# An order of instructions recomputed from other transfer times, with a margin behind landings

## The chip, the cores and the metric

The kernel runs on one core of one Trainium2 chip. The metric is the device time of one execution in microseconds; smaller is better. Three timed runs of the kernel before gave 565.68, 567.0 and 568.76 us; their median, 567.0 us, is the time before.

A core has five engines, each with an instruction queue of its own that is worked off in order: TensorE (PE in the profile, with its weight loads as PEld), VectorE (DVE), ScalarE (ACT), GpSimd (POOL) and SyncE (SP). In this kernel SP does nothing but start transfers. An instruction can wait for a semaphore; while it waits, everything behind it on the same queue waits too.

## The reference

Two equal layers on `x` of 2048 tokens by 640 features, in bfloat16. Each layer normalises, does a segmented attention with a running memory, adds, normalises, does a ReLU feed-forward of width 1728, and adds:

```
x = x + A(layernorm(x))      # 32 heads of 20, 4 segments of 512 tokens
x = x + relu(layernorm(x) @ w1) @ w2
x = x + A(layernorm(x))
x = x + relu(layernorm(x) @ w1) @ w2

# A, for each segment s with q, k, v of 32 heads:
p     = softmax(q k^T * 20**-0.5 + causal mask)
a_dot = p v
a_mem = (phi(q) M) / (phi(q) z + 1e-6)
o     = sigmoid(beta) * a_mem + (1 - sigmoid(beta)) * a_dot
M     = M + phi(k)^T v ;  z = z + sum(phi(k))       # phi(t) = t + 1 or exp(t)
out   = concat(o) @ wo
```

## The kernel before

All weights and the whole of `x` stay on the core. The work is cut by layer (2), by segment (4 of 512 tokens) and, within attention, by pairs of head groups: a group is four heads, so a segment has eight groups and four pairs, and the whole kernel has 32 pairs, counted m = 0 to 31. A pair's scores are made in five rounds of two halves each; a half fills two banks of PSUM, ACT takes the exponential of it (L1155), and POOL cuts the causal triangle (L1167). PE then multiplies by the values (L1197 in the first segment, L1246 after it). Between these, PE does the projections of later segments (L640 is the first matmul of each accumulation group, L643 the others), the reads and updates of the running memory (L996, L1047), the output projection and the feed-forward. A few matmuls of the identity (L623 at the start, L627 later) compute nothing: they keep PE's clock up where it is expected to have nothing else.

Three kinds of transfer sit between the engines, nearly all of them started from SP. Queries and keys are copied from `stg` to DRAM (`spill`, L889) and read back with heads on other partitions into one of three `pad` buffers (`fill`, L934); only the first pair is copied on the chip (`first_heads`, L913). Transposes (`turn`, L671) turn normalised tokens, attention values (`avt`), head outputs (`oT`) and `phi(k)`; SP holds its queue for each of them. The loads of the weights come in pieces (`late_loads`, L528 to L546); `w2` is loaded into a region that the first segments use for other data until their last memory read (L996 with `w_r`), so its pieces wait for that.

The order of the instructions is not written by hand. Every step is a stream that yields operations (`Op`), and `Sched.run` merges the streams when the program is built. It keeps a clock for each engine and a time for each result. In each turn it takes from the heads of all streams the one with the smallest `round(start + late)`: `start` is when the engine is free and the awaited results are there by its own costs, and `late` is a penalty that moves an operation back in the choice but not in its time. Already there before: for a PE operation of a stream that is not first in rank, a result that came from a transfer counts only 1000 ns after its recorded landing (`TRUST_NS`). Where a planned gap of PE is 300 ns or more, `keep_busy` fills it with identity matmuls. A transfer's recorded landing is the end of its issue (or the end of the transfers before it) plus `lat`.

The whole plan is made for 32 values of the assumed cost of a change of PE's tiling (`STARTS`: 97 ns, up and down in steps of 0.75). `late(seed)` then replays each order with random extra landing times (mean `LATE_NS`, 300 ns), and the order with the smallest sum over four seeds is the one that is emitted. On the chip nothing of this is left but the order on each queue and the semaphores: no instruction waits for a planned time.

Of the kernel before, what the change touches and what calls it, by code (L numbers as in the profile page):

```python
# [18 lines left out]
FC = D // 128  # L19
# [140 lines left out]
SWITCH_NS = 97.0  # L160
STARTS = [SWITCH_NS + 0.75 * (k - 32 // 2) for k in range(32)]
LATE_NS = 300.0
JOIN_NS = 4000.0
SEM_NS = 60.0
PE_MARGIN = 80.0
IDLE_NS = 300.0
COLD_NS = 8000.0
TRUST_NS = {"dma": 1000.0, "pool": 400.0, "act": 400.0, "dve": 400.0, "pe": 0.0}
# [4 lines left out]
class Sched:  # L173
# [93 lines left out]
    def run(self):  # L267
        while True:
# [22 lines left out]
            for prio, n, st, alts, op, late in heads:  # L291
# [4 lines left out]
                if prio > 0 and alts and alts[0][3] == "pe":  # L296
                    sl = self._pick(op.acq).tks if op.acq is not None else []
                    sure = max([self.at(t) + TRUST_NS[self.P.lane(t)] for t in op.waits + sl], default=0.0)
                    late = max(late, sure - alts[0][1])
                for end, start, k, e in alts:  # L300
                    if not any(p2 < min(prio, HOLDERS) and st2 is not st
                               and any(e2 == e and s2 + HOLD_TOL[e] < end for _, s2, _, e2 in al2[:1])
                               for p2, _, st2, al2, _, _ in heads):
                        ok.append((end, start, k))
# [30 lines left out]
            if op.dma is not None:  # L335
                tk = self.P.dma(e, fns[0][0], op.dma)
                self.dma_free = max(self.dma_free, start + 300.0) + tail[1]
                self.t[(id(tk[0]), tk[1])] = max(self.dma_free, end) + tail[0]
                if tail[2]:
# [13 lines left out]
    def late(self, seed):  # L353
# [5 lines left out]
        for e, hold, tail, waits, out, is_dma in self.log:  # L359
            m = SEM_NS + (PE_MARGIN if e == "pe" else 0.0)  # L360
            start = max([t[id(k[0]), k[1]] + m for k in waits], default=0.0)
            start = max(free[e], start)
            free[e] = start + hold
            if is_dma:
                dma_free = max(dma_free, start + 300.0) + tail[1]
                land = max(dma_free, free[e]) + tail[0] + rnd.expovariate(1.0 / LATE_NS)
                if tail[2]:
                    free[e] = max(free[e], dma_free)
# [39 lines left out]
def plan(switch, sb, sem_, psum, dram, A_x, A_wq, A_wk, A_wv, A_wo, A_beta, B_x, B_w1, B_w2, out):  # L408
# [86 lines left out]
    def ld(e, name, nbytes, fn, waits=()):  # L495
        tk = yield dma(e, sem_("d_" + name), nbytes, fn, waits, lat=2200.0)
        S.set(name, tks=[tk])
# [26 lines left out]
    def late_loads():  # L524
# [27 lines left out]
        for n, (name, nbytes, fn) in enumerate(pieces):  # L552
# [3 lines left out]
            if n == n2:  # L556
                v0 = yield Need("v00")
                q1 = yield Need("q01")
                w2w = v0 + q1 + early_done
            tk = yield dma("sp", sems[name], nbytes, fn, w[:1] + (w2w if n >= n2 else []) + z1, issue=400.0, lat=4500.0)  # L560
            left[name] -= 1
# [105 lines left out]

    def turn(slot_sem, dst, src, waits):

        n = src.shape[-1] // 128  # L670
        tk = yield dma("sp", slot_sem, 32768 * n, lambda e: e.dma_start_transpose(dst, src), waits,  # L671
                       issue=max(1400.0, 140.0 * n), lat=2000.0, rate=270.0, holds=True)
        return tk

    def lnorm(s, x_tks, pool_, parts=1):
# [3 lines left out]
        for p0 in range(0, 4, n):  # L679
# [11 lines left out]
            for i in range(p0, p0 + n, 2):  # L691
# [5 lines left out]
                t1 = yield dve(D, 4, lambda e, bx=bx, t=t: nm(e, bx, t, 1), [tch], extra=120)  # L697
                tT = yield from turn(xn_sem[id(bx)], xt.ap[:, i * FC:(i + 2) * FC, :], bx.ap, [t0, t1] + xt.tks)
                bx.release(tT)
# [563 lines left out]
    def turn_av(m):  # L1263
        ev = yield Need("av", m)
        sl, ev = ev[0], ev[1:]
        at = yield Acq([AVT])
        tT = yield from turn(avt_sem, at.ap, sl.ap.rearrange("p z t -> p (z t)"), ev + at.tks)
        sl.release(tT)
# [54 lines left out]
    def turn_o(a, s):  # L1323
        ow = yield Need("oseg", a, s)
        turned = []
        for k in range(2):
            ot = yield Acq([OT[k]])
            ot.users = []
            tT = yield from turn(ot_sem[id(ot)], ot.ap, o_sb[:, 2 * k:2 * k + 2, :].rearrange(
                "p i d -> p (i d)"), ow + ot.tks)  # L1330
            turned.append(tT)
# [19 lines left out]
    def ln_b(p):  # L1351
        def f(a, s):
# [18 lines left out]
            for k in range(2):  # L1371
                tk = yield normed(t0 + k, k, bx, tch)
                tn.append(tk)
            tT = yield from turn(xn_sem[id(bx)], xt.ap[:, 2 * p * FC:(2 * p + 2) * FC, :], bx.ap, tn + xt.tks)
            bx.release(tT)
# [190 lines left out]
```

## Time and profile before

| what | value |
|---|---|
| timed runs, median (lowest, highest) | 567.0 us (565.68, 568.76) |
| profiled execution, its own time | 565.3 us |
| its span, first to last instruction | 563.5 us |
| PE busy | 556.4 us (99%), 5219 matmuls |
| DVE busy | 420.1 us (75%) |
| ACT busy | 404.2 us (72%) |
| POOL busy | 195.1 us (35%) |
| granted TensorE clock | 1.000 |
| bytes moved | 60.93 MB, mean 108 GB/s |

The profiled execution is at the fast end of the runs: 1.7 us under their median. A busy PE is not PE at its peak: matmuls overlap, and a gap between two of them that is shorter than the last one takes to drain is counted as busy. So small losses of PE are read from the starts of its instructions in the timeline, and only waits that outlast the drain show as idle.

### The profile page before, as it was taken

To read this page: it belongs to the slowest core of one execution; us is meant where nothing else is said; L and a number is where in the kernel's file an instruction comes from. 1 tells how busy PE (TensorE), PEld (TensorE's weight loads), DVE (VectorE), ACT (ScalarE), POOL (GpSimd) and SP (SyncE) were. 2 spreads that over 40 slices of the span, in tenths; PEclk is the share of its full clock that TensorE was granted. 3 is DMA by queue.
4 is the path that set the end of the run, shared out by engine and by line. 5 is a ranking of instruction groups with operands and counts; after the bars stand their busy time and mean duration, and the time that the engine had idled before them with its cause. 6 is when DMAs were issued, how large, how long until landed. Compare 5 with 4: busy or idle time off the path is not lost.

```text
span 563.5 us, 12875 instructions
## 1 busy us (share of the span) xinstructions
PE 556.4 (99%) x5219; PEld 305.0 (54%) x5219; DVE 420.1 (75%) x1070; ACT 404.2 (72%) x512; POOL 195.1 (35%) x302
## 2 busy tenths in 40 slices
PE   8999999999999999999999999999999999999998
PEld 7664555445554454645446544555445654665655
DVE  6989789888999689878898997688747964560202
ACT  4789998987788878778986688778878678113140
POOL 4544344333344335444433443035322433110000
PEclk9999999999999999999999999999999999999999
DMA  8695988383474136542375131880326410512101
GB/s 268 120 221 138 238 218 182 74 224 56 97 171 94 44 88 159 118 95 72 92 163 115 27 66 26 193 148 20 67 80 173 109 43 20 116 45 48 47 1 47
DMA packets 130109, 60.93 MB, mean 108 GB/s; under 512 B 108930, under 2 KB 119938, under 8 KB 130050
## 3 DMA queue, kind: packets, MB, share of 16 engines
q1 hardware_dynamic: 129830, 59.85, 45.5%
q8 instruction: 41, 0.67, 0.5%
q10 hardware_dynamic: 220, 0.26, 0.2%
q14 instruction: 18, 0.15, 0.1%
HBM read 20.57 MB, written 12.85 MB: 59 GB/s over the span
## 4 chain that ended last, share of the span: by engine, by line
PE 87%; DVE 8%; DMA 2%; ACT 1%; SPq 1%; issue 0%
PE ps L643 56%; PE ps L640 11%; PE ps L1103 8%; PE ps L1246 6%; DVE stats L651 2%; PE ps L996 2%; PE ps L1197 1%; PE ps L1047 1%; DVE x_sb L1317 1%; PE ps L1394 1%; DMA avt<-av 1%; DVE xn_tok L705 1%; SPq L913 1%; DMA oT<-o_sb 1%; ACT PT L1155 1%; DVE stg L816 1%
## 5 line engine op out<-in xcount | busy, mean ns | idle before, releaser
L1155 ACT ACTIVATE PT<-ps 128x1024 bf16<-128x1024 f32 x320 | 310.0, 1022 | 70.3 <-PE ps L1103 64.6
L1167 POOL TENSOR_SCALAR_AFFINE_SELECT PT<-PT 128x512 bf16<-128x512 bf16 x256 | 166.6, 668 | 268.2 <-ACT PT L1155 267.9
L643 PE MATMUL ps<-w_r,hT 128*128 128x320 bf16 (+2 forms) x768 | 123.0, 299 | 0.0
L643 PE MATMUL ps<-xnT,w_r 128*128 128x512 bf16 x416 | 113.3, 379 | 0.0
L1317 DVE TENSOR_TENSOR x_sb<-x_sb,ps 128x320 bf16<-128x320 bf16 (+1 forms) x128 | 60.3, 479 | 66.7 <-PE ps L643 66.0
L643 PEld LDWEIGHTS ps<-w_r,hT 128*128 128x128 bf16 x768 | 72.4, 98 | 31.9 <-issue 4.4
L1425 ACT ACTIVATE hT<-ps 128x512 bf16<-128x512 f32 x55 | 32.7, 598 | 50.0 <-PE ps L643 49.7
L1103 PE MATMUL ps<-pad 20*128 20x128 bf16 (+3 forms) x1024 | 64.8, 301 | 1.6 <-ACT PT L1155 0.9
L643 PEld LDWEIGHTS ps<-xnT,w_r 128*128 128x128 bf16 x416 | 39.7, 98 | 44.0 <-issue 3.2
L651 DVE BATCH_NORM_STATS2 stats<-x_sb 128x6 f32<-128x320 bf16 x126 | 56.4, 472 | 2.1 <-DMA x_sb<-in_A_x_dram 1.8
L1254 DVE CAST av<-ps 128x512 bf16<-128x512 f32 x53 | 36.2, 684 | 14.8 <-PE ps L1246 14.7
L1103 PEld LDWEIGHTS ps<-pad 20*128 20x128 bf16 x1024 | 18.3, 92 | 52.6 <-ACT PT L1155 25.6
L643 PE MATMUL ps<-wo_r,oT 128*128 128x320 bf16 x256 | 46.1, 299 | 0.0
L1246 PE MATMUL ps<-PT,v_aug 128*32 128x256 bf16 (+5 forms) x896 | 40.7, 302 | 0.0
L1423 DVE TENSOR_SCALAR hT<-ps 128x512 bf16<-128x512 f32 x49 | 33.4, 683 | 9.1 <-PE ps L643 9.0
L640 PE MATMUL ps<-xnT,w_r 128*128 128x512 bf16 x104 | 39.6, 380 | 0.0
L643 PE MATMUL ps<-wv_r,xnT 128*128 128x320 bf16 x192 | 36.7, 300 | 0.0
L643 PE MATMUL ps<-xnT,wk_r 128*128 128x512 bf16 (+1 forms) x140 | 36.1, 349 | 0.0
L643 PE MATMUL ps<-xnT,wq_r 128*128 128x512 bf16 (+1 forms) x140 | 34.9, 349 | 0.0
L665 POOL TENSOR_TENSOR rstd<-lnU,mhalf 128x2 f32<-128x2 f32 (+2 forms) x25 | 20.8, 831 | 38.0 <-DVE lnU L661 34.4
L816 DVE CAST stg<-ps 128x512 bf16<-128x512 f32 (+1 forms) x48 | 29.5, 618 | 3.3 <-PE ps L643 3.2
L1290 DVE TENSOR_TENSOR o_sb<-avt,rden 128x320 bf16<-128x320 bf16 x56 | 30.5, 562 | 0.6
(117 smaller groups left out, 695.8 us busy)
## 6 DMA issues: line engine op xcount, KB each, us to landing
pad<-scr SPq DMA_DIRECT2D x124, 80.0 KB
scr<-stg SPq DMA_DIRECT2D x34, 256.0 KB, 2.9
out_dram<-x_sb SPq DMA_DIRECT2D x15, 160.0 KB, 1.8
w_r<-in_B_w_dram SPq DMA_DIRECT2D x10, 216.0 KB, 4.2
w_r<-in_B_w_dram SPq DMA_DIRECT2D x13, 160.0 KB, 2.8
x_sb<-in_A_x_dram SPq DMA_DIRECT2D x9, 160.0 KB, 2.8
scr<-w_r SPq DMA_DIRECT2D x5, 256.0 KB, 3.6
x_sb<-in_A_x_dram SPq DMA_DIRECT2D x3, 320.0 KB, 7.2
```

The costliest lines, as they stand in the source:

```text
L640: bk, tk = yield pe(mm_ns(n), [(lambda e, bk, a=a, b=b: e.matmul(bk.ap[:, 0:n] if len(b.shape) == 2 else bk.ap[:, 0:n].rearrange("p (i n) ...
L643: tk = yield pe(mm_ns(n), [(lambda e, k=k, a=a, b=b, bk=bk: e.matmul(bk.ap[:, 0:n] if len(b.shape) == 2 else bk.ap[:, 0:n].rearrange("p (i ...
L651: tk = yield dve(320, 1, lambda e, c2=c2: e.bn_stats(stats6[:, t, c2, :], x_sb[:, t, c2 * 320:(c2 + 1) * 320]), xt)
L816: te = yield evac(N, 1, lambda e, sg=sg, bk=bk: e.tensor_copy(sg.ap[:, t0:t0 + N], bk.ap[:, 0:N]), lambda e, sg=sg, bk=bk: e.activation(sg ...
L1103: fns.append([(lambda e, z=z, j=j, hh=hh, N=N, o=o, sl=sl: e.matmul(ps[:, hh, o:o + N], sl.ap[32 * hh:32 * hh + DH, z, 0, 128 * j:128 * j ...
L1155: tx = yield act(1024, lambda e, dst=dst, src=src: e.activation(dst, src, ACT.Exp, scale=SCALE), sc + pw)
L1167: tm = yield pool(600.0, lambda e, reg=reg: e.affine_select(out=reg, in_=reg, pattern=[[0, 4], [1, 128]], compare_op=ALU.is_ge, fill=0.0, ...
L1246: fns.append((lambda e, bk, j=j, hh=hh, pt=pt, g=g0 + z: e.matmul(bk.ap[32 * hh:32 * hh + wide(g, hh), 128 * j:L], VAUG[vx(a, s)][:, j].re ...
L1254: te = yield evac(L, 1, lambda e, sl=sl, z=z, bk=bk: e.tensor_copy(sl.ap[:, z], bk.ap), lambda e, sl=sl, z=z, bk=bk: e.activation(sl.ap[:, ...
L1317: ta = yield dve(n, 1, lambda e: e.tensor_tensor(x_sb[:, t, c0:c0 + n], x_sb[:, t, c0:c0 + n], bk.ap[:, 0:n], ALU.add), [tk] + list(waits) ...
L1423: th = yield evac(512, 1, lambda e, dc=dc, bk=bk: e.tensor_scalar(hT[:, dc, :], bk.ap[:, :], 0.0, None, ALU.max), lambda e, dc=dc, bk=bk: ...
L1425: lambda e, dc=dc, bk=bk: e.activation(hT[:, dc, :], bk.ap[:, :], ACT.Relu), [tk] + HT.tks)
```

## The change

Only numbers of the planner change, and what it does with them; no step of the computation is added or removed.

- Transfer times: the loads at the start get a `lat` each (1500 to 3800 ns, where all had 2200), the late pieces 3500 instead of 4500, the transposes of normalised tokens and of head outputs 2400 and those of attention values 1600, where all had 2000.
- A transfer started between 8 and 106 us is recorded as landing 600 ns later (`EARLY_NS`), and the random replay adds a further random delay of that mean to it.
- A margin: where the first choice of engine of an operation is ACT or DVE and it waits for a transfer, it is penalised in the choice if it would start less than 800 ns (`SURE_NS`) behind the recorded landing.
- The replay charges 1000 ns (`COOL_NS`) for each wait of PE of over 800 ns after the first 10 us.
- The plans tried are 48 instead of 32.

```diff
-STARTS = [SWITCH_NS + 0.75 * (k - 32 // 2) for k in range(32)]
+STARTS = [SWITCH_NS + 0.75 * (k - 48 // 2) for k in range(48)]
+SURE_NS = 800.0
+EARLY_NS = 600.0
+LOADS_NS = 106e3
+COOL_NS = 1000.0
...
+                if alts and alts[0][3] in ("act", "dve"):
+                    sure = max([self.at(t) for t in op.waits if self.P.lane(t) == "dma"], default=0.0)
+                    late = max(late, sure + SURE_NS - alts[0][1])
...
-                self.t[(id(tk[0]), tk[1])] = max(self.dma_free, end) + tail[0]
+                self.t[(id(tk[0]), tk[1])] = max(self.dma_free, end) + tail[0] + (EARLY_NS if 8e3 < start < LOADS_NS else 0.0)
...
+            if e == 'pe' and start - free[e] > 800.0 and start > 10e3:
+                start += COOL_NS
...
+                if 8e3 < start < LOADS_NS:
+                    land += rnd.expovariate(1.0 / EARLY_NS)
...
-        tk = yield dma(e, sem_("d_" + name), nbytes, fn, waits, lat=2200.0)
+        tk = yield dma(e, sem_("d_" + name), nbytes, fn, waits, lat={"x0a": 1950.0, "x0b": 1950.0, "x01": 1500.0, "wk0": 2900.0, "wq0": 2900.0, "wk1": 2900.0, "wq1": 2500.0, "wv": 2200.0, "x10": 3800.0, "x11": 3800.0}.get(name, 2200.0))
...
-            tk = yield dma("sp", sems[name], nbytes, fn, w[:1] + (w2w if n >= n2 else []) + z1, issue=400.0, lat=4500.0)
+            tk = yield dma("sp", sems[name], nbytes, fn, w[:1] + (w2w if n >= n2 else []) + z1, issue=400.0, lat=3500.0)
...
-                tT = yield from turn(xn_sem[id(bx)], xt.ap[:, i * FC:(i + 2) * FC, :], bx.ap, [t0, t1] + xt.tks)
+                tT = yield from turn(xn_sem[id(bx)], xt.ap[:, i * FC:(i + 2) * FC, :], bx.ap, [t0, t1] + xt.tks, lat=2400.0)
...
-        tT = yield from turn(avt_sem, at.ap, sl.ap.rearrange("p z t -> p (z t)"), ev + at.tks)
+        tT = yield from turn(avt_sem, at.ap, sl.ap.rearrange("p z t -> p (z t)"), ev + at.tks, lat=1600.0)
```

The transposes in `turn_o` and `ln_b` get `lat=2400.0` in the same way. The lines of the kernel after stand 11 further down than those of before.

More of the change, by code (lines that the diff above doesn't have):

```diff
@@ L666, in chain, with turn @@
         return tk
-    def turn(slot_sem, dst, src, waits):
+    def turn(slot_sem, dst, src, waits, lat=2000.0):
         n = src.shape[-1] // 128
         tk = yield dma("sp", slot_sem, 32768 * n, lambda e: e.dma_start_transpose(dst, src), waits,
-                       issue=max(1400.0, 140.0 * n), lat=2000.0, rate=270.0, holds=True)
+                       issue=max(1400.0, 140.0 * n), lat=lat, rate=270.0, holds=True)
         return tk
@@ L1329, in turn_o @@
             tT = yield from turn(ot_sem[id(ot)], ot.ap, o_sb[:, 2 * k:2 * k + 2, :].rearrange(
-                "p i d -> p (i d)"), ow + ot.tks)
+                "p i d -> p (i d)"), ow + ot.tks, lat=2400.0)
             turned.append(tT)
@@ L1373, in f @@
                 tn.append(tk)
-            tT = yield from turn(xn_sem[id(bx)], xt.ap[:, 2 * p * FC:(2 * p + 2) * FC, :], bx.ap, tn + xt.tks)
+            tT = yield from turn(xn_sem[id(bx)], xt.ap[:, 2 * p * FC:(2 * p + 2) * FC, :], bx.ap, tn + xt.tks, lat=2400.0)
             bx.release(tT)
```

## The prediction

> **What bounds the kernel now.** I read the page first, then the table of stages, then who waited for whom on PE, then the timeline.
>
> ```profile
> PE 556.4 (99%) x5219; PEld 305.0 (54%) x5219; DVE 420.1 (75%) x1070; ACT 404.2 (72%) x512; POOL 195.1 (35%) x302
> PE 87%; DVE 8%; DMA 2%; ACT 1%; SPq 1%; issue 0%
> ```
>
> PE is busy nearly always and carries 87% of the chain that ended last; transfers carry 2%. The work of PE is the same before and after, so the order can only change what PE loses between its matmuls.
>
> ```profile
> 19.30:80.00 60.70, 60.63 (x740) 34.91 (x740) 54.11 (x148) 55.59 (x74) 26.34 (x39) 1.00 0.82 196
> 80.00:105.10 25.10, 24.05 (x258) 13.37 (x258) 22.62 (x65) 22.57 (x29) 10.57 (x18) 1.00 0.80 168
> 183.00:480.00 297.00, 296.73 (x2763) 153.48 (x2763) 233.87 (x576) 236.61 (x288) 113.88 (x173) 1.00 0.40 91
> ```
>
> Columns after the stage's length: busy PE, PEld, DVE, ACT, POOL, granted clock (1.00: full), DMA share, GB/s. From 183 us on PE idles 0.27 us in 297. The one stage with a visible loss behind the start is 80 to 105 us (1.05 us idle), where DVE and ACT are 90% busy.
>
> ```profile
> PE ps L1103 <- ACT PT L1155: 0.9, 3, 0.4
> PE ps L1103 <- DMA pad<-stg: 0.6, 1, 0.6
> PE ps L640 <- DVE av L1254: 0.4, 2, 0.2
> PE ps L996 <- DVE om_sb L1007: 0.2, 1, 0.2
> PE ps L640 <- DMA oT<-o_sb: 0.2, 1, 0.2
> ```
>
> These are all waits of PE from 12 us to the end: 2.3 us, of which transfers 0.8. That is all that truer transfer times can win outright, 0.4% of 565.
>
> **The prices of PE's order**, from the timeline (start, length, what):
>
> ```profile
> 76.77 0.71 PE L1197 MATMUL ps<-w_r,PT 128*128 128x21 bf16 x22
> 77.55 1.02 PE L643 MATMUL ps<-hT,wq_r 128*128 128x512 bf16 x4
> 78.51 0.39 PE L1103 MATMUL ps<-pad 20*128 20x256 bf16 x4
> 78.83 0.39 PE L640 MATMUL ps<-hT,wq_r 128*128 128x512 bf16 x1
> 80.34 1.40 PE L627 MATMUL ps<-ident 128*128 128x128 bf16 x22
> 84.00 0.31 PE L640 MATMUL ps<-wo_r,oT 128*128 128x320 bf16 x1 [0.21 <-DMA oT<-o_sb]
> ```
>
> Four matmuls of 512 columns, 1.02 us with a last one of 0.38: a step of (1.02 - 0.38)/3 = 0.21 us. The last starts at 77.55 + 0.64 = 78.19, the scores at 78.51, 0.32 later: the change of tiling costs about 0.10. The way back: two runs of 256 columns, at half of 0.21 each, 0.21 together, and 0.32 until 78.83: again 0.10. Filling matmuls: 22 in 1.40 us, and 0.219 for one alone, (1.40 - 0.22)/21 = 0.056 each.
>
> **The change, part by part.** It adds no instruction of work, no wait and no transfer; all its terms come from comparing the two orders, which I did by counting, without times from the planner.
>
> *Fills and tilings.* Behind the start (from the first value projection on) the order before has 39 filling matmuls, the one after 56: 22 and 6 near 80 us, 3 near 113, 8 near 450 become 15 and 14 near 105, 6 near 131, 3, and 18 near 460. Seventeen more at 0.056 are **+0.95 us**; PE runs them whether or not what follows is late. Changes of tiling rise from 393 to 399: six at 0.10, **+0.6 us**. Neither has cover: both stand on PE.
>
> *The start.* These are the rows that it rests on.
>
> ```profile
> 8.08 0.70 POOL L765 TENSOR_TENSOR rstd<-lnU,mhalf 128x2 f32<-128x2 f32 x1 [1.11 <-DVE lnU L763]
> 8.24 0.49 DVE L734 COPY xnT<-ps 128x640 bf16<-128x640 bf16 x1 [0.24 <-PE ps L728]
> 8.88 0.27 PE L640 MATMUL ps<-xnT,wk_r 128*128 128x256 bf16 x1
> 8.98 0.60 PE L643 MATMUL ps<-xnT,wk_r 128*128 128x256 bf16 x4
> 10.03 0.44 PE L728 MATMUL ps<-ident,xn_tok 128*128 128x128 bf16 x5
> 12.78 1.42 DVE L956 TENSOR_SCALAR rtmp<-stg 128x512 bf16<-128x512 bf16 x1 [1.78 <-ACT stg L817]
> 13.02 1.04 POOL L586 MEMSET maskg<- 128x756 bf16 x1
> 13.80 0.30 PE L640 MATMUL ps<-wv_r,xnT 128*128 128x320 bf16 x1
> 14.12 0.41 DVE L816 CAST stg<-ps 128x256 bf16<-128x256 f32 x1
> 14.62 4.73 SPq L913 DMA_DIRECT2D pad<-stg  x6
> 18.41 0.27 PE L640 MATMUL ps<-xnT,wk_r 128*128 128x256 bf16 x1
> 19.30 0.40 PE L1103 MATMUL ps<-pad 20*128 20x512 bf16 x4 [0.62 <-DMA pad<-stg]
> ```
>
> Before, PE starts projecting at 8.88, between the transposes of the second two tiles (the last at 10.03). After, all four transposes stand ahead of the first projection, and on DVE the statistics of tile 3 stand ahead of the first normalisation. The second pair is bound by the same `rstd` (8.78) and one copy (0.49), so its last transpose still comes at about 10; eight groups of five steps of (0.60 - 0.27)/3 = 0.11, 4.4 us, then end at 14.6 to 14.7 instead of 13.80: 0.86 late. Fifteen fills that stood ahead of 8.88 are gone, but PE waits there instead.
>
> Most of it comes back at the first scores. Before, PE has 36 matmuls from 13.80 on, the last at 18.41 lasting a step of 0.11, so it loses 0.78 until the scores at 19.30, whose operands come by transfers issued from 14.62 on. After, 42 matmuls stand there, 5.3 us, and PE arrives at about 19.95. Those transfers do not move as PE does: their issue waits for the cast at 14.12, which is behind a 1.42 us `rtmp`, which ends 0.14 behind POOL's memset. The memset starts as before, so I put the issue at 14.75 and the operands at 19.4: nothing is lost. Net: 0.86 - 0.78, **+0.1 us**. What the old wait hid: nothing late is behind it, since the read-back of the first pair's second half is first asked for some 4 us later.
>
> ```profile
> L956 DVE TENSOR_SCALAR rtmp<-stg x50: 223/285/1423, 12.8 to 433.7; 128x512 bf16<-128x512 bf16 x50
> ```
>
> The same instruction takes 285 ns at the median and 1423 once, beside that memset. The Trainium skill (SBUF — State Buffer, section "SBUF: two separate sides") says that such a VectorE instruction and GpSimd share a port pair as an exclusive lock, held for the whole instruction. By that rule the start follows POOL and the issue is at 14.75; if instead the 1.42 us were its own, all would shift by 0.86, the operands would be there at 20.15, and 0.2 us more would be lost. The row fits the rule, and the sum above does not need it: it takes the end of the memset from the rows.
>
> *The load stage, 20 to 106 us.* Every in-order exponential on ACT stands between PE and its next score bank.
>
> ```profile
> 19.72 1.94 ACT L1155 ACTIVATE PT<-ps 128x1024 bf16<-128x1024 f32 x2 [1.12 <-PE ps L1103]
> 21.55 0.45 ACT L868 ACTIVATE w_r<-ps 128x320 bf16<-128x320 f32 x1
> 21.86 0.64 ACT L963 ACTIVATE phs<-stg 128x512 bf16<-128x512 bf16 x1
> 24.79 0.39 ACT L817 ACTIVATE stg<-ps 128x256 bf16<-128x256 f32 x1
> 25.05 0.64 ACT L963 ACTIVATE phs<-stg 128x512 bf16<-128x512 bf16 x1
> 25.57 1.95 ACT L1155 ACTIVATE PT<-ps 128x1024 bf16<-128x1024 f32 x2
> ```
>
> From start to start: two exponentials 1.83, a value cast 0.31, a small cast 0.26, a phi exponential 0.52. Counting both orders for the first pair of head groups (first exponential to the eleventh): before ten exponentials, 4, 1 and 3 of the others, 12.2 us; after 3, 3 and 3, 12.4. PE's own steps from the first score of this pair to that of the next add up to 14.0 before and 13.0 after. For pair 4 they are 12.3 before and 12.4 after, and ACT's share goes from 4 phi exponentials (11.2) to 5 and two casts (12.4). ACT has no slack left there. Bounds: it costs nothing if ACT runs without a gap, and 1.9 us if it idles as in the row of 19.3 to 80 us (5.1 of 60.7, 8.4%: 12.4/0.916 is 13.5 against 13.0 and 12.4, so 0.6 and 1.1, and pair 3, with 12.1 against 13.1, 0.1). I take **+0.4 us**, near the lower end, because that stage shows PE waiting for 0.07 us in all.
>
> *The wait for `oT` at 84.00 goes.* Its matmul stands 8.7 us of PE's steps behind the last values of the segment (L1197), where before it was reached 6.7 us behind them on the clock (they end their issue at about 77.3): **-0.2 us**. The 80 to 105 us stage else keeps its late casts (DVE and ACT decide them), so I leave its loss as it is; next late there is `av` on DVE.
>
> *SP's queue.* The transposes' and pieces' places move. The heaviest move: ten of `w2`'s pieces went out together before, ahead of one attention transpose and one of `phi(k)`; after, all but the last go ahead of them.
>
> ```profile
> 114.12 4.62 SPq L532 DMA_DIRECT2D w_r<-in_B_w_dram  x10
> 132.03 0.30 PE L640 MATMUL ps<-w_r,hT 128*128 128x320 bf16 x1
> w_u<-in_B_w_dram SPq DMA_DIRECT2D x1, 80.0 KB, 3.7
> 124.42 0.59 SPq L546 DMA_DIRECT2D w_u<-in_B_w_dram  x1
> ```
>
> The last piece landed at 124.42 + 3.7 = 128.1 and was used at 132.03: 3.9 us of slack. After, PE has about 2.7 us fewer steps from the last memory read of that region to this matmul: 1.2 us are left. **0.** The transpose behind four more pieces of 0.46 is up to 1.8 us later, and only a division on DVE reads it.
>
> *Sum.* 0.95 + 0.6 + 0.1 + 0.4 - 0.2 = +1.85 us on the profiled 565.3 (span 563.5 and 1.8 around it): 567.1. The median of the runs lies 1.7 above that execution, so against it I say **568.8 us**, 0.3% above 567.0, within the 0.5% (2.8 us) that a measurement here can tell from no change.
>
> **The rivals.**
> - *The margin pays (0.14).* Waits for transfers and what follows them vanish, in slow runs as in fast ones: all 2.3 us of waits above less the 0.8 already counted, and the 1.7 us between profile and median: 568.8 - 0.4 - 1.5 - 1.7 = 565.2. For it: the runs spread by 3 us. Against it: only 0.8 of the waits name a transfer. It ends below 564.2 only with a better start too.
> - *ACT decides the load stage (0.26): slower.* The idle time of the row of 19.3 to 80 us is needed in each pair: 1.9 instead of 0.4, **570.3**, and with the spread of the runs up to 572. It decides from about 1.4 us on. For it: zero slack in pair 4; against it: PE's 0.07 us of idle there before.
> - *`w2` or a transpose late behind SP (0.07).* Once the 1.2 us are used, each us later is a us of PE; with the 1.8 us behind four pieces on top of a wait as long as the slack, some 570.5.
> - *The clock falls (0.03).* The start shows the price:
>
> ```profile
> 1.58 4.28 PE L623 MATMUL ps<-ident 128*128 128x128 bf16 x43 [1.58 <-POOL mhalf L576]
> ```
>
> 43 matmuls at (4.28 - 0.31)/42 = 0.095 instead of 0.056: 1.7 us. With a wait longer than any in the trace (over 0.7) that is 571.5 or more. The Trainium skill (TensorE: Matmul & The Clock Gate, section "Part 1: The HAM clock gate") puts the re-throttling behind an idle window of about 3.4 us; by that page the time would be some 574. No wait of the trace comes near it, and the clock column of the stages agrees.
> - *The orders do not differ where it counts*: excluded, they differ nearly throughout.
>
> **How the numbers follow.** The forecast itself has 0.50. It ends within 0.5% mostly (0.39), else slower (0.10). The margin paying gives 0.10 same and 0.04 faster; ACT 0.05 same and 0.21 slower; the others 0.10 slower. Faster 0.05, same 0.54, slower 0.41. Range: from 565.2, the first rival, to 572.5, ACT's upper end and the clock's; the likeliest alone 566.5 to 570.5.
>
> **What would show it.** First value projection near 14.6 us and no wait at the first scores; 56 fills behind it; no wait for `oT`; PE waiting for L1155 near 75 to 90 us at most some tenths; the `w2` matmul without a wait. I am wrong if PE's waits behind 12 us sum to under 1 or over 4 us, or the start is not later.

## The result, and the profile after

The kernel after takes 569.01 us (median of 10 runs, 567.63 to 569.91), the kernel before 566.22 in the runs beside it. The ratio is 1.0044, with a 95% interval of 1.003 to 1.0057: by that, 2.5 us (0.44%) slower. The profiled execution of the kernel after spans 567.3 us, 3.8 more than the profiled one of before (563.5).

Page of the kernel after: busy time of the engines, the queue of instruction packets (packets, MB, share), the chain that ended last.

```profile
PE 557.2 (98%) x5223; PEld 305.4 (54%) x5224; DVE 415.1 (73%) x1067; ACT 405.6 (72%) x515; POOL 194.7 (34%) x302
q8 instruction: 41, 0.67, 0.5%
PE 80%; DVE 12%; DMA 3%; ACT 3%; issue 1%; SPq 0%; POOL 0%
```

PE still carries the chain, but its share falls from 87 to 80% and DVE's rises from 8 to 12%. The next two fences give the table of stages of after and, for those stages that were not shown before, of the kernel before (columns as in the prediction).

```profile
80.00:106.00 26.00, 25.96 (x268) 13.82 (x266) 24.90 (x71) 23.30 (x31) 11.12 (x18) 1.00 0.70 178
106.00:183.00 77.00, 75.20 (x720) 38.07 (x717) 63.78 (x164) 62.31 (x74) 32.31 (x48) 1.00 0.52 119
183.00:250.00 67.00, 65.70 (x647) 34.38 (x648) 55.49 (x139) 52.14 (x62) 26.44 (x40) 1.00 0.43 94
250.00:480.00 230.00, 228.76 (x2119) 118.51 (x2118) 177.99 (x446) 181.92 (x223) 85.43 (x133) 1.00 0.42 91
```

```profile
106.00:183.00 77.00, 76.56 (x750) 39.22 (x748) 69.99 (x181) 62.52 (x74) 31.37 (x48) 1.00 0.55 122
183.00:250.00 67.00, 66.77 (x636) 34.26 (x639) 54.18 (x128) 53.90 (x65) 29.36 (x43) 1.00 0.42 96
250.00:480.00 230.00, 229.96 (x2131) 119.22 (x2124) 179.70 (x449) 182.71 (x224) 84.52 (x130) 1.00 0.39 90
```

PE's idle time at 80 to 106 us falls from 1.05 to 0.04 us; at 106 to 480 us it rises from 0.71 to 4.34. The waits of PE in the kernel after, from 12 us to the end (total, times, longest):

```profile
PE ps L1058 <- DMA phk<-phs: 1.2, 1, 1.2
PE ps L651 <- DMA xnT<-xn_tok: 0.9, 1, 0.9
PE ps L1114 <- ACT PT L1166: 0.8, 2, 0.6
PE ps L1114 <- DMA pad<-scr: 0.6, 1, 0.6
PE ps L651 <- issue: 0.5, 1, 0.5
PE ps L1007 <- DVE om_sb L1018: 0.4, 1, 0.4
PE ps L1007 <- DVE av L1265: 0.4, 1, 0.4
```

They sum to 4.8 us, where before had 2.3; 2.7 of them name a transfer, where before had 0.8.

Idle time misses losses shorter than a matmul's drain, so below I use *PE's loss*. From the starts of its matmuls in the trace, it takes every step that exceeds the usual step of its kind (0.21 us for 512 columns, and so on; a change of tiling 0.10 more) by over 0.15 us, and adds up the excess. What is left, the usual steps with excesses too small to tell from them, is *PE's stream*. From the first value projection, which starts at 13.80 us in both kernels, to the end:

```
us                        before   after   difference
PE's stream                                  +0.49
loss, 13.8 to 20 us         0.68    0       -0.68
loss, 20 to 80 us           0       0.69    +0.69
loss, 80 to 106 us          1.55    0.20    -1.35
loss, 106 us to the end     1.11    5.73    +4.62
sum                                          +3.77
```

With all the small excesses counted as loss too, the stream's difference becomes 0.3 to 0.8 us, by what is taken as usual; the rows keep their signs. So ahead of 106 us, where the new transfer times and their 0.6 us apply, PE's loss became smaller by 1.3 us; much more than that came behind it. The recorded expectations below count the small excesses as well, and so speak of 5 us for the kernel before and 7 for the one after, where this count gives 3.3 and 6.6.

**Where the 4.6 us are.** Timeline of the kernel after around the largest loss (1.6 us in two pieces), and the transfers that were issued from 176 to 183 us (last column: us from issue to landing):

```profile
174.31 3.43 SPq L682 DMA_TRANSPOSE xnT<-xn_tok  x2
177.78 1.52 SPq L682 DMA_TRANSPOSE avt<-av  x1
181.65 0.39 PE L651 MATMUL ps<-xnT,wk_r 128*128 128x512 bf16 x1 [0.92 <-DMA xnT<-xn_tok]
182.33 0.35 DVE L1293 RECIPROCAL rden<-avt 128x32 f32<-128x32 bf16 x1 [2.21 <-DMA avt<-av]
```

```profile
q8 instruction: 1, 0.02, 0.8%
xnT<-xn_tok SPq DMA_TRANSPOSE x1, 5.2
avt<-av SPq DMA_TRANSPOSE x1, 4.5
```

The second of the two `xnT` transposes took 5.2 us to land, the `avt` transpose 4.5. PE waits for the first. DVE stands 2.21 us in front of a division for the second, and what is queued behind that division on DVE is late for PE 0.8 us later (0.4 for `om_sb`, in the list above; 0.56 by the steps). In the same stretch lies one packet of queue q8, 0.02 MB. Every trace of this study has 41 of these, 16 KB each, one for about every 251 instructions of PE (matmuls and weight loads) in the mean; in the kernel after they took 0.9 to 1.9 us each. Sorting the transposes behind 106 us of all fourteen traces by whether a packet was under way in the second half of their usual time (the median of their kind):

```
median us, issue to landing   no packet then (count)   packet under way (count)
avt<-av                       2.73 (294)               4.26 (81)
oT<-o_sb                      3.12 (157)               4.66 (39)
xnT<-xn_tok                   3.56 (265)               4.59 (43)
phk<-phs                      4.08 (73)                5.15 (25)
```

A packet is not the only way to be late: of the 294 `avt` transposes without one, 26 landed over 1 us behind the usual, of the 81 with one, 63. The page also has a second queue of instruction packets, q14 (18 of 8 KB); the 7 `avt` transposes that met only one of those took 3.56 us at the median. This became the leading theory (F): the loss behind 106 us comes of transposes that meet such a packet close to where PE or DVE needs them. Where the packets fall goes by the number of PE's instructions (experiment 1), so every order has others, and the planner knows nothing of them. Its rival is theory P: the planner put the readers too near behind their transposes, packets or not. The other large loss, 1.4 us at 228 us, has a second way in it:

```profile
219.41 3.37 SPq L945 DMA_DIRECT2D pad<-scr  x4
224.76 1.92 SPq L682 DMA_TRANSPOSE phk<-phs  x1
229.49 0.58 PE L1058 MATMUL ps<-v_aug,phk 128*128 128x147 bf16 x6 [1.21 <-DMA phk<-phs]
```

A packet started at 219.88. The four read-backs held SP for 3.37 us, one of them, issued at 220.37, alone for 2.04 (0.33 to 0.62 each where no packet was near, in experiment 1), and the transpose for PE's memory update came later by that. The `issue` wait in the list seems to belong here too: its matmul, at 166.29 us, reads `xnT`, and an `xnT` transpose issued at 161.00 landed at 166.2, beside a packet. So 3.6 of the 5.7 us stand at three places with a packet.

### The profile page after: what moved, and what is told of

It reads as the page before. It is cut to its first block, busy times and chain, and to the rows that moved or that the text cites. A ratio compares the mean times of both kernels' runs of the same rounds, so it can differ in the third digit from the quotient of the medians.

```text
span 567.3 us, 12876 instructions
## 1 busy us (share of the span) xinstructions
PE 557.2 (98%) x5223; PEld 305.4 (54%) x5224; DVE 415.1 (73%) x1067; ACT 405.6 (72%) x515; POOL 194.7 (34%) x302
## 4 chain that ended last, share of the span: by engine, by line
PE 80%; DVE 12%; DMA 3%; ACT 3%; issue 1%; SPq 0%; POOL 0%
PE ps L654 52%; PE ps L651 10%; PE ps L1114 8%; PE ps L1257 5%; DVE stats L662 2%; PE ps L1007 2%; ACT PT L1166 2%; DVE x_sb L1328 1%; DMA avt<-av 1%; PE ps L1208 1%; DVE stg L827 1%; PE ps L1058 1%; DMA phk<-phs 1%; PE ps L1405 1%; DVE xn_tok L716 1%; DVE xn_tok L704 1%
## 5 line engine op out<-in xcount | busy, mean ns | idle before, releaser
L1436 ACT ACTIVATE hT<-ps 128x512 bf16<-128x512 f32 x58 | 34.7, 599 | 51.4 <-PE ps L654 51.1
L1114 PE MATMUL ps<-pad 20*128 20x384 bf16 (+3 forms) x1024 | 64.1, 301 | 1.6 <-ACT PT L1166 0.8
L1434 DVE TENSOR_SCALAR hT<-ps 128x512 bf16<-128x512 f32 x46 | 31.3, 681 | 11.2 <-PE ps L654 11.1
L654 PEld LDWEIGHTS ps<-wo_r,oT 128*128 128x128 bf16 x256 | 24.4, 98 | 11.6 <-issue 2.7
```

What stands on the lines that cost most here:

```text
L654: tk = yield pe(mm_ns(n), [(lambda e, k=k, a=a, b=b, bk=bk: e.matmul(bk.ap[:, 0:n] if len(b.shape) == 2 else bk.ap[:, 0:n].rearrange("p (i ...
L1114: fns.append([(lambda e, z=z, j=j, hh=hh, N=N, o=o, sl=sl: e.matmul(ps[:, hh, o:o + N], sl.ap[32 * hh:32 * hh + DH, z, 0, 128 * j:128 * j ...
L1434: th = yield evac(512, 1, lambda e, dc=dc, bk=bk: e.tensor_scalar(hT[:, dc, :], bk.ap[:, :], 0.0, None, ALU.max), lambda e, dc=dc, bk=bk: ...
L1436: lambda e, dc=dc, bk=bk: e.activation(hT[:, dc, :], bk.ap[:, :], ACT.Relu), [tk] + HT.tks)
```

## The experiments

All times are medians beside runs of the kernel before on the same chip (566.0 to 566.6 us), ratios with 95% intervals; the ratios are not the quotients of the medians, and differ from them by up to a quarter of a percent. Each kernel has one trace. Where a planner's starting price is fixed in an edit, the order is the one that the kernel's own planner picks, or the one named.

**1. The same order, with the packets moved.** The 43 identity matmuls of the start become 11 of 512 columns, so 64 instructions of PE fewer stand ahead of everything; all else keeps its order.

```diff
-            ps[:, 0, 0:128], ident[:], ident[:], start=True, stop=True), k == 42) for k in range(43)], idt)
+            ps[:, 0, :].rearrange("p (i n) -> p i n", n=128), ident[:], ident[:][:, None, :].to_broadcast([128, 4, 128]), start=True, stop=True), k == 10) for k in range(11)], idt)
```

On the kernel after:

> The changed kernel's order with the 43 identity matmuls of the start made as 11 of 512 columns (they compute nothing, so the output stays): 64 instructions of PE fewer ahead of everything, all else in the same order. Theory F: every instruction packet comes about 3.4 us later against the order; the transposes at 176 and 218 us land without one (3.5 instead of 5.2 us), the waits at 180 and 228 us go, and the time falls by up to 3 us if no other place is hit: 0.998 to 1.004 of the kernel before. Theory P: the waits and the time stay as they are in the changed kernel, 1.003 to 1.006.

Measured: 567.77 us, ratio 1.0023 (1.0009 to 1.0037), although its first value projection comes 0.33 us later (14.12). The same place of its timeline, and the transfers issued from 176 to 183 us:

```profile
178.18 1.42 SPq L682 DMA_TRANSPOSE avt<-av  x1
180.97 0.38 PE L651 MATMUL ps<-xnT,wk_r 128*128 128x512 bf16 x1
181.14 0.35 DVE L1293 RECIPROCAL rden<-avt 128x32 f32<-128x32 bf16 x1 [0.62 <-DMA avt<-av]
```

```profile
xnT<-xn_tok SPq DMA_TRANSPOSE x2, 3.4
avt<-av SPq DMA_TRANSPOSE x1, 2.9
```

The order is the same, the packet comes later, at 182.8, the transposes land in 3.4 and 2.9 us, and both waits of PE, for `xnT` and for `om_sb`, are gone; so is most of the one at 228 us (1.38 to 0.20). The 0.62 at 166 us is gone too, but there PE now waits for ACT instead: 0.79 at 168 us, where the kernel after had 0.17. A new one is 0.78 at 428 us. What no packet made stays: 0.53 at 297 us in both, and near 360 us 0.48 of 0.69. PE's loss falls from 6.6 to 4.5 us in all. On the kernel before:

> The kernel before with its 43 identity matmuls of the start made as 11 of 512 columns (output unchanged), all else in the same order. Theory F: the packets at 162 and 189 us, which coincide with the attention transposes that land after 4.3 and 4.4 us, come 3.4 us later; those two land after about 2.7, and PE's losses near 166 (0.5) and 195 us (0.4) go unless others are hit: 0.997 to 1.002. Theory P: both landings and losses stay, 0.999 to 1.001.

Measured: 567.53 us, 1.002 (1.0006 to 1.0035), of which 0.42 us is the later start. The transposes at 162 and 188 us land in 3.2 and 2.7 us, as theory F said (before 4.3 and 4.4). The loss at 195 us (0.40) goes with them; the one at 166 (0.51) stays, a wait for ACT, so there the theory was wrong. Losses appear or grow at 129 (0.37), 200 (0.43, behind two `oT` transposes of 4.9 us beside a packet), 296 and 361 us; 5.0 us in all, before 3.3. The same edit makes one kernel faster and the other slower. It shows, with the order held, that the packets move losses of 0.3 to 1.2 us about; the kernel before lost less with its own places than with these.

**2. Without the filling matmuls.** The order is kept; only the identity matmuls behind the start go.

```diff
-        if gap < IDLE_NS or self.idle_fn is None:
+        if gap < IDLE_NS or self.idle_fn is None or self.free["pe"] > 10e3:
```

On the kernel after (56 fills, 3.1 us):

> The order of the changed kernel without its 56 filling matmuls behind the first 10 us (29 near 105, 6 near 131, 3 near 226, 18 near 460 us); all else stands in the same order. The identity matmuls compute nothing, so the output stays. Theory F (the fetch): the late landings that PE waited for at 180 and 228 us in the changed kernel are those of transposes that coincide with a 16 KB packet of the instruction queue, which comes once in some 252 instructions of PE; without 35 fills (70 instructions) it comes some 3.7 us later against the order, so both waits (1.1 and 0.6 near 181, 1.4 at 228) go or shrink under 0.4, besides half to all of the fills' 56 x 0.056 = 3.1 us: 3 to 6 us faster than the changed kernel, 0.992 to 0.999 of the kernel before. Theory P (the planner put the readers too near behind their transposes): both waits stay, only fills are won: 1.5 to 3.1 us, 0.999 to 1.002.

Measured: 566.66 us, 1.0000 (0.9984 to 1.0015): 2.3 us faster than the kernel after. That is not the price of fills. Where 29 of them stood (80 to 106 us, 1.6 us), PE's loss rises from 0.20 to 1.39; where the last 18 stood (1.0 us), it now waits 0.92. So 2.1 of these 2.6 us come back as waits. The larger part of the gain is again that packets moved: the losses at 180 and 228 us shrink from 1.6 and 1.4 us to 0.25 and 0.22, though 0.57 appears at 250 us. The ratio is in the range of theory P and misses that of theory F, which had half of the fills or more as gain; the two waits did what theory F says. On the kernel before (39 fills):

> The kernel before without its 39 filling matmuls behind the first 10 us (28 near 80, 3 near 113, 8 near 450 us), all else in the same order; output unchanged. If fills are a pure cost, 39 x 0.056 = 2.2 us faster: 0.996. If PE waits in their place for ACT near 80 us, 0.5 us or less: 0.999 to 1.000. If the clock falls without them, slower. Theory F adds that packets behind 80 us come 3 us later, which moves late landings to other transposes, either way by up to 2 us; theory P expects no landing to change.

Measured: 568.81 us, 1.0045 (1.0029 to 1.0061): slower. Its table of stages:

```profile
82.00:85.00 3.00, 1.79 (x27) 0.67 (x27) 1.65 (x5) 3.00 (x5) 1.84 (x3) 1.00 1.04 232
85.00:90.00 5.00, 5.00 (x26) 2.75 (x27) 2.64 (x8) 3.24 (x5) 1.36 (x3) 0.66 0.95 190
```

PE loses 1.36 and 0.51 us where the fills were, and then the granted clock falls: 0.66 in the mean of 85 to 90 us, and under 1.000 over the whole execution in all twelve runs. The fills are worth what they cost there. This trace also shows how far two executions of one order can differ: ahead of any fill that was dropped, an instruction packet started at 24.93 us, where the trace of before has one at 25.43; the `hT` transpose issued at 21.9 landed after 5.45 us instead of 3.61, and PE lost 0.76 us at 27.5 us that it did not lose before.

**3. The two halves of the change apart.** The margin is these lines; the first kernel is the one after without them, the second the one before with them. Both planners choose anew.

```diff
+                if alts and alts[0][3] in ("act", "dve"):
+                    sure = max([self.at(t) for t in op.waits if self.P.lane(t) == "dma"], default=0.0)
+                    late = max(late, sure + SURE_NS - alts[0][1])
```

> The changed kernel without the margin that ACT and DVE keep behind transfers; the corrected transfer times stay, and the planner finds its own order with them. That order has 25 filling matmuls behind the first value projection (the changed kernel 56, before 39) and 399 changes of tiling (399, 393), so PE's own stream is 1.5 us shorter than that of the changed kernel and 0.4 shorter than before. Theory M (the margin is what costs): PE's waits fall to those of before as well, 5 us instead of 7, and the ratio to before is 0.999 to 1.001. Theory T (the new transfer times cost, with or without a margin): waits stay near 7 us or above, ratio 1.002 to 1.004. Theory F (the loss behind 106 us is decided by which transposes meet an instruction packet of PE close to where PE needs them, which is another draw in every order): waits of 0.5 to 1.4 us stand again behind 106 us, but at other places than 180 and 228, and each of them follows a transpose that landed 1.5 us later than its like; the ratio may be anywhere from 0.998 to 1.006.

Measured: 566.05 us, 0.999 (0.9978 to 1.0001), the ratio of theory M. PE's loss is 4.2 us. Three waits of 0.7 to 0.8 us remain. The one at 408.9 us, for a cast on DVE, stands behind an `avt` transpose that met a packet (issued at 403.37, 4.51 us to landing). The one at 426 us is for read-backs issued right behind another such transpose (420.23, 4.41 us). For the one at 99.5 us there is no packet: it belongs to the late casts of the load stage. So theory F holds behind 106 us only, and for two of three waits.

> The kernel before with the margin alone, and its old transfer times. Its order has 33 filling matmuls and 399 changes of tiling, and a stream of PE 0.2 us longer than before. Theory M: waits of PE as in the changed kernel, about 7 us, ratio 1.003 to 1.005. Theory T: waits as before, 5 us, ratio 0.999 to 1.002. Theory F: no rule on the size; the waits above 0.5 us behind 106 us each follow a transpose that landed late beside an instruction packet.

Measured: 571.12 us, 1.007 (1.0046 to 1.0094), above what theories M and T gave. There are six runs; three at full clock took 568.5, 569.1 and 571.4 us, three at 0.997 took 570.8 to 572.6. The trace is the one of 571.4. PE's loss is 9.5 us in it, and 4.8 of that lies at 20 to 106 us. The first of PE's waits and, in the second fence, its timeline:

```profile
PE ps L644 <- DMA hT<-xn_tok: 3.1, 3, 1.4
```

```profile
23.35 3.71 SPq L675 DMA_TRANSPOSE hT<-xn_tok  x2
28.04 0.30 PE L644 MATMUL ps<-wv_r,hT 128*128 128x320 bf16 x1 [1.32 <-DMA hT<-xn_tok]
57.71 2.20 SPq L675 DMA_TRANSPOSE hT<-xn_tok  x1
63.88 0.31 PE L644 MATMUL ps<-wv_r,hT 128*128 128x320 bf16 x1 [1.44 <-DMA hT<-xn_tok]
```

Timeline of the kernel before, the same transposes:

```profile
21.75 3.05 SPq L671 DMA_TRANSPOSE hT<-xn_tok  x2
53.46 1.77 SPq L671 DMA_TRANSPOSE hT<-xn_tok  x1
```

The order with the margin sends these transposes 1.6 us later at the first pair and 4.3 us later at the other. Without its wait PE would have come to them only 0.3 us later than before at the first (26.7 against 26.4 us) and 2.4 at the other (62.4 against 60.0), where the landing also took 6.1 us instead of 4.5, beside a packet. None of the four orders with the corrected times (this experiment and the next) waits for a transposed `hT`, and both with the old times and the margin do: that the corrected times take this price away is likely, but argued from these few orders.

**4. Is it the margin, or the draw of one order?** The order that each planner ranks second, by fixing its starting price.

```diff
-STARTS = [SWITCH_NS + 0.75 * (k - 48 // 2) for k in range(48)]
+STARTS = [94.75]
```

The kernel after:

> The changed kernel with the order that its planner ranks second (another starting price, 94.75 instead of 103.0); margin and corrected times are the same. 50 filling matmuls, 396 changes of tiling, PE's stream 0.1 us shorter than in the changed kernel. Theory M (the margin is what costs the 3 us between the changed kernel and the one without the margin): waits of PE about 7 us again, ratio to before 1.003 to 1.006. Theory D (each order is a draw: which late transposes stand close to PE decides): the waits are anywhere from 4 to 9 us and stand at other places than 180 and 228 us; a ratio outside 1.003 to 1.006 speaks for it.

Measured: 569.03 us, 1.0043 (1.0025 to 1.0062), inside what theory M gave. The loss is 5.7 us, at 102 to 104 (1.8), 184 (1.7) and 200 us (1.0): other places than in the kernel after. In the profiled execution 1.6 us come on top by a fall of the clock (last section), which most of the timed runs do not have. Timeline at 184 us: an `avt` transpose issued at 178.10 landed in 4.6 us beside a packet,

```profile
182.73 0.35 DVE L1293 RECIPROCAL rden<-avt 128x32 f32<-128x32 bf16 x1 [1.84 <-DMA avt<-av]
185.75 0.56 PE L1257 MATMUL ps<-PT,v_aug 128*32 128x512 bf16 x8 [1.63 <-DVE v_aug L878]
```

DVE stood in front of the division, and the cast of the values that PE needs was queued behind it. Without the margin, starting price 85.75:

> The kernel with the corrected times and without the margin, with the order that its planner ranks second. 43 filling matmuls, 402 changes of tiling, PE's stream 1.3 us longer than that of its first choice. Theory M: waits as in the first choice, 5.5 us, so 1.3 us above it: ratio 1.000 to 1.002. Theory D: waits of 4 to 9 us, ratio 0.998 to 1.007.

Measured: 569.11 us, 1.0035 (1.0016 to 1.0054), above what theory M gave; loss 6.7 us, 2.5 more than its first choice. The two largest stand in its timeline at 359.5 and 398.2 us:

```profile
359.52 0.39 PE L1111 MATMUL ps<-pad 20*128 20x512 bf16 x4 [1.30 <-DMA pad<-scr]
398.24 0.34 PE L1004 MATMUL ps<-BD,stg 128*128 128x147 bf16 x3 [1.28 <-DVE om_sb L1015]
```

The second follows an `avt` transpose (391.91, 4.67 us to landing) beside a packet; beside the read-backs of the first the trace has none. The kernel before with the margin, starting price 88.75:

> The kernel before with the margin alone, second choice of its planner. 71 filling matmuls, 397 changes of tiling, PE's stream 1.7 us longer than that of the first choice with the margin. If the old transfer times are what brings the 5.4 us of waits at 20 to 80 us (three of them for a transposed operand of the projections) once DVE keeps a margin: waits there again of 4 us or more, ratio 1.007 to 1.012. If that was the draw of one order: waits there under 2.5 us, ratio 1.001 to 1.006.

Measured: 571.51 us, 1.0074 (1.0045 to 1.0102). The ratio is that of the first expectation; the loss at 20 to 80 us is 2.1 us (3.1 with the small excesses, as the expectation counts), where that one asked for 4 or more. One wait of 0.9 us for `hT` is left in it, so about half of this price was the draw of one order. Medians together:

```
us                              first choice   second choice
old times, no margin (before)      566.5            -
old times, margin                  571.1          571.5
new times, no margin               566.05         569.1
new times, margin (after)          569.0          569.0
```

On the old times the margin costs 4.6 and 5.0 us by the medians (4.0 and 4.2 by the ratios; six runs each, and half of the first six had a lower clock), and the new times take back some 2 us. On the new times it costs 3 us by the first choices and nothing by the second; two orders of one rule lie 3 us apart. That the margin costs time on the new times is therefore not shown, and I leave it open. What is shown is that the planner's ranking does not see differences of this size.

**5. Later landings behind 106 us.** Every transpose recorded 1.6 us later:

```diff
         n = src.shape[-1] // 128
+        lat += 1600.0
```

> The changed kernel with the landing of every transpose recorded 1.6 us later, which is what a transpose beside an instruction packet takes longer; the planner finds its own order. 73 filling matmuls, 397 changes of tiling, PE's stream 0.8 us longer than in the changed kernel. If late transposes are the cause of the loss behind 106 us and a truer landing mends it: no wait above 0.3 us for a transposed operand there, waits 4 to 5 us in all, ratio to before 1.000 to 1.002. If the order simply draws new collisions and PE has no other work to put in their place: waits of 7 us and the ratio 1.004 to 1.008.

Measured: 568.39 us, 1.0034 (1.0024 to 1.0045), between the two expectations; loss 4.2 us. No wait for a transposed operand is left, as expected, and DVE no longer waits for `avt` at all; but a wait of 1.3 us for ACT at 176 us and 73 fills stand in their place. Then the 0.6 us of the load stage for all transfers to the end:

```diff
-LOADS_NS = 106e3
+LOADS_NS = 600e3
```

> The changed kernel with the 0.6 us that it adds to the landings of the load stage (8 to 106 us) added to all transfers to the end. 94 filling matmuls, 400 changes of tiling, PE's stream 2.5 us longer than in the changed kernel. If the loss behind 106 us comes of landings recorded too early there: waits behind 106 us fall from 5.5 to about 2 us, which pays for the stream, ratio 1.002 to 1.005. If not: waits as in the changed kernel, and the fills come on top, ratio 1.007 to 1.010.

Measured: 568.02 us, 1.0028 (1.0015 to 1.0042). It has the smallest loss of all, 2.8 us, with 0.9 behind 106 us (5.7 after), and its two longest waits are these:

```profile
PE ps L1058 <- DMA phk<-phs: 0.9, 1, 0.9
PE ps L651 <- DVE v_aug L878: 0.3, 1, 0.3
...
```

DVE's waits for `avt` fall to 1.5 us; in the kernel after they are 5.9, in the one without the margin 9.2. So later recorded landings do remove waits. But PE's stream grew by some 2.5 us over the kernel after, mainly by 38 more fills (2.1 us; 94 in all, 5.3 us): the planner, which had believed that PE had work, now plans gaps. Without these fills, in the same order:

> The changed kernel with 0.6 us added to all transfers to the end, in the same order as in the earlier run of it, without the 94 filling matmuls behind the start (5.3 us of PE). If PE waits where the fills stood, as it did when the changed kernel lost its 56: half of the 5.3 us comes back as waits, 2.5 us are gained, ratio 1.000 and no lower than 0.998. If the fills stood for transfers and casts that are there in time: ratio 0.994 to 0.997, faster than both kernels. If a wait is long enough for the clock to fall, as in the kernel before without its fills (granted clock 0.66 at 85 to 90 us): 2 us more, ratio 1.003 to 1.005, with a granted clock under 0.9 in one stretch between 100 and 140 us.

Measured: 570.64 us, 1.005 (1.0028 to 1.0071): slower still. Of the 5.3 us, 5.1 come back as loss in its profiled execution, at full clock (7.9 against 2.8 us), and in most of its runs the clock fell as well (last section). DVE's waits for `avt` are back at 7.0 us in it, with the same order. The gaps were real, and the fills in them had kept waits away.

No kernel beat the one before beyond what can be measured; the one with the new times and no margin, in its first order, equals it.

## Why the prediction came out

The forecast of 568.8 us lies 0.2 from the median, and the change of 0.44% is a loss inside the 0.5%, as forecast. By its own tests the working was not: PE's waits sum to 4.8 us, where over 4 was to mean wrong, and the start is not later, where that too was to mean wrong. The predicted sum of +1.85 us on the profiled execution measured +3.77 there, and it came about by terms that mostly had other sizes. That the median is met all the same is luck: the forecast adds 1.7 us to the sum, the distance of the profiled execution of before (565.3) from the median of three runs. By ten runs that distance is 0.9 (566.22), and for the kernel after it is nothing (569.11 in the profile, 569.01 in the median). The 1.7 us took the place of the 1.9 that the sum lacks.

- *Fills and changes of tiling, +1.55.* The counts were right (56 and 399), but PE's stream measured +0.5 (0.3 to 0.8); which steps made up for the rest is not traced. What failed is "neither has cover": experiment 2 shows that 2.1 of 2.6 us of fills stand where PE would have waited. They are waits by another name.
- *The start, +0.1: failed, −0.7.* The step that failed is "the second pair is bound by the same `rstd` (8.78)", and with it "the memset starts as before". Timeline of the kernel after:

```profile
7.41 0.84 POOL L776 TENSOR_TENSOR rstd<-lnU,mhalf 128x2 f32<-128x2 f32 x1 [0.35 <-DVE lnU L774]
8.79 0.81 PE L739 MATMUL ps<-ident,xn_tok 128*128 128x128 bf16 x10 [0.19 <-DVE xn_tok L716]
...
12.41 1.04 POOL L597 MEMSET maskg<- 128x756 bf16 x1
12.78 0.82 DVE L967 TENSOR_SCALAR rtmp<-stg 128x512 bf16<-128x512 bf16 x1 [3.01 <-ACT stg L828]
13.80 0.30 PE L651 MATMUL ps<-wv_r,xnT 128*128 128x320 bf16 x1
14.01 3.19 SPq L924 DMA_DIRECT2D pad<-stg  x4
19.20 0.40 PE L1114 MATMUL ps<-pad 20*128 20x512 bf16 x4
```

  With the statistics of tile 3 ahead of the first normalisation, `rstd` ends at 8.25 instead of 8.78; I had moved the DVE work and kept the time of what depends on it. All transposes end at 9.6, the eight groups take the 4.4 us that I had counted, and the first value projection starts at 13.80, as before. The memset ends 0.61 us earlier, the `rtmp` beside it ends 0.15 behind it (before 0.14), and the transfers go out at 14.01 instead of 14.62. PE reaches the scores at 19.20 with six more matmuls done and no wait. That `rtmp` now takes 0.82 us instead of 1.42 and again ends just behind the memset settles the two readings that I gave: it is not its own length. The Trainium skill (SBUF — State Buffer, section "SBUF: two separate sides") has the shared port pair locked for a whole instruction, and both rows agree.
- *The load stage, +0.4 for ACT and −0.2 for `oT`: +0.7 and −1.35.* The wait for `oT` is gone, as said. ACT's missing slack did cost something, at one place; before, PE had no such loss at 20 to 80 us. Timeline of the kernel after:

```profile
73.19 0.39 PE L1114 MATMUL ps<-pad 20*128 20x512 bf16 x2 [0.63 <-ACT PT L1166]
```

  So this term had the right cause and nearly the right size. "I leave its loss as it is", for 80 to 106 us, is the step that failed: 1.55 became 0.20, with 29 fills standing at 101 to 105 us, and without them it is 1.39 (experiment 2).
- *`w2`, 0: right.* The first matmul of that region, at 129.47 us, has no wait.
- *Behind 106 us, nothing: +4.6.* This is the step that decided the size. I bounded what transfers do by the waits of the profile of before, and took it that an order with the same transfers would have the same ones. Those 1.1 us were what one order had drawn. In the new order four transposes meet a packet within 60 us, issued at 161.0, 176.4, 177.8 and 217.75 us, landing in 5.2, 5.2, 4.5 and 5.3 us.
- *The rivals.* The margin did not pay at PE. DVE's waits for `avt` fit it on the new times (9.2 us in both orders without, 5.9 and 6.6 with it), but moved packets alone took 5.9 to 2.3 (experiment 1), and before, without a margin, it was 6.7. ACT cost the load stage 0.7 us, not the 1.9 of its rival, `w2` was not late, and the clock was 1.00 in every stage shown. None of the rivals decided the time; a late transpose appears in one of them, but behind SP, not beside a packet.

So the number was right by luck: of −1.3 us ahead of 106 us and +4.6 behind it the sum had next to nothing, and the 1.7 us of the median stood in for what it lacked.

## What to carry to other kernels

The waits of one order are a sample, not a property: with a planner that reorders everything, take the spread between orders of the same rules (here up to 3 us, 0.5%) as an uncertainty of the forecast, and judge a rule by several orders. When PE is nearly always busy, a safer landing time trades a wait for a planned gap, and the fill matmuls make that gap look like work, so count fills and waits together. When a step moves on one engine, recompute the times of everything that depends on it before calling a later step bound by it.

## What the runs showed of the hardware

*Instruction packets and transposes.* 41 packets of 16 KB, one per about 251 instructions of PE, go with a landing that is 1.0 to 1.5 us later for a transpose under way (table above); the same order with the packets elsewhere loses the waits that stood there. The prediction left queue q8 out, whose share is 0.5%.

*The clock falls without a whole idle window.* Table of stages of the second-choice order of the kernel after:

```profile
102.50:105.00 2.50, 0.87 (x21) 0.43 (x18) 2.50 (x8) 2.35 (x3) 1.03 (x3) 1.00 0.83 170
105.50:108.50 3.00, 3.00 (x34) 2.71 (x27) 1.94 (x7) 2.46 (x3) 0.60 (x2) 0.50 0.39 87
```

PE worked 0.87 of 2.5 us, in pieces, and from about 105.2 to 108.7 us its clock was half. In experiment 2 the granted clock fell in the same way, behind losses of 1.36 and 0.51 us. In the clock records of these two traces the half speed lasts 3.41 us both times, and the full speed ahead of it 98.99 and 78.51 us, which are 29 and 23 times that; so the clock seems to be set anew on a grid of 3.41 us. In the 3.41 us ahead of the two falls PE was busy for 1.78 and 2.08 us. A busy share alone does not tell: the second-choice order had another such stretch, from 183.8 us, with PE as little busy (1.78 us), and the clock stayed. What decides is open. The Trainium skill (TensorE: Matmul & The Clock Gate, section "Part 1: The HAM clock gate") names an idle window of about 3.4 us; the time at half speed agrees with that length, the full idleness does not, and my rival on the clock should have asked for less than that. The price is read from the twelve runs of the order with 0.6 us on all transfers and no fills, which lie in three groups:

```
mean granted clock   runs   us
1.000                  2    567.4 to 567.7
0.997                  3    568.8 to 569.5
0.994                  7    570.6 to 571.1
```

Each step of 0.003 in the mean clock is 1.7 us of 569, half of 3.4 us, and costs that in the time.
